# The first layer's two-bank PSUM tile as two one-bank tiles, with every ELU pass done by halves

## The chip, the cores and the metric

One NeuronCore of one Trainium2 chip runs the whole program. A core has five engines with in-order instruction queues of their own: TensorE (PE, matrix multiplication), VectorE (DVE), ScalarE (ACT), GpSimd (POOL) and SyncE (SP, which here only issues DMAs). They meet through semaphores. PE writes its results into PSUM, which has eight banks; a bank holds 512 fp32 values in each of 128 partitions. The metric is the device time of one execution in microseconds (us), the median over repeated runs without a profiler.

## The reference

The input x has 8 batches of 3008 rows and 256 columns. Two parts follow each other.

```
X  = rfft(x, axis=1)                    # along the 3008 rows
Yr = Xr @ w_r - Xi @ w_i + b_r ;  Yi = Xr @ w_i + Xi @ w_r + b_i
Y  = soft threshold of both parts by 0.01
y  = irfft(Y)                           # [8, 3008, 256]

h  = y.reshape(24064, 256) @ w_in       # [24064, 2048], the first layer
g  = where(h > 0, h, exp(min(h, 0)) - 1)  # ELU
out = g @ w_out                         # [24064, 256], the second layer
```

The change lies wholly in the second part: in where h stands in PSUM, and in how the ELU is cut into instructions.

## The kernel before

The Fourier transforms are matrix multiplications in two stages each way, cut into small pieces called units. Unit A is the first stage of the forward transform, X the second, M the complex weights with bias and threshold, B and Y the two stages back. Each unit is a handful of matmuls into PSUM and an evacuation to SBUF by ACT or DVE (line 144 for DVE, line 146 for ACT, in the helper `evac`); M units also use POOL (lines 301 to 303).

The two dense layers are one long loop of 376 steps (line 1207), 47 for each batch. The 24064 rows are taken in blocks of 512 (`TB`), and a block's 2048 hidden columns in eight pairs of 128-column tiles. Step i has these parts:

- `front(i)`: the first layer of one pair. Four bf16 matmuls (line 1006), two for each 128-column tile, write `hps`, a PSUM tile of two banks with one 128-column tile in each. Then ACT computes the exponential of h into `Et` in SBUF.
- `finish_elu()` for the step before: DVE joins `Et` and h to `gT` (line 1048 or 1050). This is the last reader of `hps`, so it frees the banks.
- `elu(i)`: for some steps POOL or DVE limits `Et` (lines 1059 and 1061).
- `back(i - 2)`: the second layer of the pair of two steps earlier, eight fp32 matmuls (line 1080) into `ps_o`. After the eighth pair the block is copied out (line 1092) and stored.

In between, a plan (`plan`, line 1110) places the units of the next batch, one a step, ahead of `front` in the same step (list `f0`) or after `finish_elu` (list `f1`). So the order in every queue is fixed by the program text: PE does unit, first layer, second layer; DVE does the unit's evacuation, then gT of the step before; ACT does the unit's evacuation, then the exponential. Nothing is reordered by a scheduler.

The ELU comes in three ways, chosen by the step's mode:

- "act" steps (130 of them, among them all with M units): ACT computes Relu(-h) into `Et` (line 1024), then Exp(-Et) in place (line 1025), each over both tiles in one instruction of 1024 elements a partition; gT is one DVE instruction of 1024.
- pooled steps (217, among them the first ten, `FILL`, and the calm ones without units): ACT computes Exp by halves of 512 (line 1022), POOL limits each half (line 1059), gT is two DVE instructions of 512.
- plain steps (29): ACT computes Exp over 1024 (line 1027), DVE limits it (line 1061), gT is one DVE instruction of 1024 (line 1050).

PSUM has eight banks: two for `ps_o`, four for `psH` (two tiles of two banks, used in turn), and two that are lent, through `last_banks`, either to the pool `psF` (one two-bank tile for A, X, B and Y units) or to `psM` (two one-bank tiles, for M units). When a calm stretch has no units, every third step's `hps` goes into these last two banks, from `psF` ("third"). The first ten steps are an exception: their h stands in two one-bank tiles `sps`, and each half's Exp is written right behind its own two matmuls (line 1013).

```
hps = psH.tile([P, 2, TB], F32, name="hps", tag="hps")          # line 994
...
nc.scalar.activation(E_, hps[:], AF.Relu, scale=-1.0)           # line 1024
nc.scalar.activation(E_, E_, AF.Exp, scale=-1.0)                # line 1025
...
nc.vector.scalar_tensor_tensor(o, e, -1.0, h, ALU.add, ALU.max) # line 1048
```

Of the kernel before, what the change touches and what calls it, by code (L numbers as in the profile page):

```python
# [8 lines left out]
ALU = mybir.AluOpType  # L9
AF = mybir.ActivationFunctionType  # L10
BF16 = mybir.dt.bfloat16
F32 = mybir.dt.float32
# [17 lines left out]
def kernel(  # L30
# [11 lines left out]
    nc = tc.nc  # L42
    P = nc.NUM_PARTITIONS
# [33 lines left out]
    space = constp.tile([P, 384], BF16, name="space")  # L77
# [13 lines left out]
    TB = 512  # L91
# [4 lines left out]
    n = B * PER  # L96
# [29 lines left out]
    def last_banks(name):  # L126

        if name not in open_pool:
            for _, stack in open_pool.values():
                stack.close()  # L130
            open_pool.clear()
            stack = ctx.enter_context(ExitStack())
            pool = stack.enter_context(
                tc.tile_pool(
                    name=name, bufs=1 if name == "psF" else 2,
                    space=bass.MemoryType.PSUM, reuse_waits="tile",
                )
            )
            open_pool[name] = pool, stack
        return open_pool[name][0]  # L140
# [91 lines left out]
    def three_weights(c, dt):  # L232

        v, r = (w[:, dt, D * c : D * c + D] for w in (wcat_s, wcat_r))
        a, b_ = (r, v) if c else (v, r)
        nc.gpsimd.tensor_tensor(v, a, b_, ALU.subtract)
# [174 lines left out]
    def two_banks(pool, n):  # L411
        return [pool.tile([P, 512], F32, name=n, tag=n) for _ in range(2)]
# [149 lines left out]
    with tc.tile_pool(name="stagep", bufs=1) as stagep:  # L562
# [3 lines left out]
        def col(eng, src, s1, op0, s2=None, op1=None, n=1, dt=F32):  # L566
            t = stagep.tile([P, n], dt, name=f"c{len(cols)}")
            cols.append(t)
            if op1 is None:
                eng.tensor_scalar(t[:], src[:], s1, None, op0)  # L570
            else:
                eng.tensor_scalar(t[:], src[:], s1, s2, op0, op1)
            return t

        def mix(eng, a, sc, b, op0, op1, n=1):
            t = stagep.tile([P, n], F32, name=f"c{len(cols)}")
            cols.append(t)
            eng.scalar_tensor_tensor(t[:], a[:], sc, b[:], op0, op1)
            return t
# [81 lines left out]
        c1 = mix(dve, qcol, -2.0, pcol, ALU.mult, ALU.add)  # L661
        c0 = col(dve, c1, -1.0, ALU.mult, 1.0, ALU.add)
# [307 lines left out]
    FILL = 10  # L970
# [5 lines left out]
    def pieces(t, k):  # L976

        out_, c = [], 0
        while c < k:
            b, r = divmod(t + c, S)  # L980
            e = min(k, c + S - r)
            out_.append((b, r, c, e))
            c = e
        return out_

    def front(i, third, on_act, halves):
        blk, fp = divmod(i, NPAIR)
        early = i < FILL
        if early:
            hps = two_banks((psS0, psS1)[i % 2], "sps")  # L990
        elif third:
            hps = last_banks("psF").tile([P, 2, TB], F32, name="hps", tag="fps")
        else:
            hps = psH.tile([P, 2, TB], F32, name="hps", tag="hps")
        todo = []
        for s in range(2):
            ft = 2 * fp + s
            for piece in sorted(pieces(blk * TB, TB), key=lambda z: z[3] - z[2]):
                todo.append((s, ft, piece))
        if i == PER // NPAIR * NPAIR:  # L1000
            todo.sort(key=lambda z: z[2][0])
        Et = late3.tile([P, 2, TB], F32, name="Et", tag="Et")
        E_ = Et[:]
        for s, ft, (b, t0, c0, c1) in todo:
            for dt in range(2):
                nc.tensor.matmul(  # L1006
                    hps[s][:, c0:c1] if early else hps[:, s, c0:c1],
                    lhsT=w_in_s[:, dt, ft * P : ft * P + P],
                    rhs=yT_of[b][:, dt, t0 : t0 + c1 - c0],
                    start=(dt == 0), stop=(dt == 1),  # L1010
                )
            if early and (dt, c1) == (1, TB):
                nc.scalar.activation(E_[:, s], hps[s][:], AF.Exp)
        if early:
            return hps, Et
        if i == n - 1:
            for h in range(2):
                t = slice(TB // 2 * h, TB // 2 * h + TB // 2)
                nc.scalar.activation(E_[:, :, t], hps[:, :, t], AF.Exp)
        elif halves:  # L1020
            for s in range(2):
                nc.scalar.activation(E_[:, s], hps[:, s], AF.Exp)  # L1022
        elif on_act:
            nc.scalar.activation(E_, hps[:], AF.Relu, scale=-1.0)  # L1024
            nc.scalar.activation(E_, E_, AF.Exp, scale=-1.0)  # L1025
        else:
            nc.scalar.activation(E_, hps[:], AF.Exp)  # L1027
        return hps, Et

    late_elu = []  # L1030
    np_all = (slice(0, P), slice(0, 2), slice(0, TB))

    def parts(i):

        if i == n - 1:
            return [
                (slice(0, P), slice(0, 2), slice(h, h + TB // 2)) for h in (0, TB // 2)
            ]
        return [(slice(0, P), s, slice(0, TB)) for s in range(2)]

    def finish_elu():
        for i, hps, Et, whole, halves in late_elu:
            gT = late3.tile([P, 2, TB], F32R, name="gT", tag="gT")
            for s in parts(i) if halves else (np_all,):
                h = hps[s[1]][:] if i < FILL else hps[s]
                o, e = gT[s], Et[s]
                if whole:
                    nc.vector.scalar_tensor_tensor(o, e, -1.0, h, ALU.add, ALU.max)  # L1048
                else:
                    nc.vector.scalar_tensor_tensor(o, h, 0.0, e, ALU.max, ALU.add)  # L1050
            g_of[i] = gT
        late_elu.clear()

    def elu(i, hps, Et, on_pool, on_act):

        E_ = Et[:]
        if on_pool:
            for s in parts(i):
                nc.gpsimd.tensor_scalar(E_[s], E_[s], 1.0, 0.0, ALU.min, ALU.max)  # L1059
        elif not on_act:  # L1060
            nc.vector.tensor_scalar(E_, E_, 1.0, -1.0, ALU.min, ALU.add)
        late_elu.append((i, hps, Et, on_pool or on_act, on_pool))

    def back(i, split):
        blk, fp = divmod(i, NPAIR)
# [140 lines left out]
    early_h = None  # L1206
    for i in range(n + LAG):
        if i == FILL:
            few.close()
            psH = ctx.enter_context(  # L1210
                tc.tile_pool(
                    name="psH", bufs=2, space=bass.MemoryType.PSUM, reuse_waits="tile"
                )
            )
        if i == LAG:
            back(0, False)
        if early_h:
            h, on_act = early_h, False
        elif i < n:
            r = i % PER  # L1220
            if r == 0:
                f0, f1, mode = plan(i // PER)
                used = [bool(u0 or u1) for u0, u1 in zip(f0, f1)]
            free = not used[r]
            bare = bare + 1 if free else 0
            calm = free and (i >= n - 2 or (r + 2 < PER and not used[r + 1] and not used[r + 2]))
            for f, a in f0[r]:
                f(*a)
            if mode[r]:
                on_act = mode[r] == "act"  # L1230
                pooled = not on_act
            else:
                on_act = any(f is unit_M for f, a in f0[r])
                pooled = free or i < FILL
            third = calm and bare % 3 == (2 if i // PER == B - 1 else 1)
            h = front(i, third, on_act, pooled)
        finish_elu()
        if i < n:
            for f, a in f1[r]:
                f(*a)  # L1240
            split = i > LAG and (i - LAG) % NPAIR == NPAIR - 1
            if split:
                back(i - LAG, True)
            elu(i, *h, pooled, on_act)
            if PER <= i < PER + 4:
                three_weights(*divmod(i - PER, 2))
            if 1 <= i < 5:
                if i < 3:
                    scale_w_in(2, True, i - 1)
                scale_w_in(3, False, (i - 1) // 2, (i - 1) % 2)  # L1250
            if i == n - 2:
                early_h = front(n - 1, True, False, True)
            elif early_h:
                early_h = None
        else:
            split = False
        if i > LAG and not split:
            back(i - LAG, False)
# [30 lines left out]
```

## Time and profile before

| what | value |
|---|---|
| median of 3 runs without a profile | 894.95 us (894.54 to 895.38) |
| span of the profiled execution, first to last instruction | 903.9 us |
| PE matmul busy | 891.3 us (99%), 6917 matmuls |
| PE weight loads busy | 675.2 us (75%) |
| DVE busy | 679.6 us (75%), 969 instructions |
| ACT busy | 722.4 us (80%), 1001 instructions |
| POOL busy | 596.7 us (66%), 806 instructions |
| mean granted PE clock | 0.948 |

The profile is of one execution; its only time on record is the span, which is longer than the runs without a profile. Busy time of PE is the union of its matmuls' modelled durations, which overlap: a matmul of 512 columns is listed with 390 ns, though the next one may start earlier. In the rows of the timeline the columns are the start and the duration in us, the engine, the source line, the operation, what it writes and reads, how many equal instructions in a row are merged, and in brackets the idle time of the engine before it with what ended it. In the rows of the groups, the number behind "x" is the count, then come busy time in us, mean ns of one instruction, and idle time ahead of them with its causes.

### The profile page before, as it was taken

How to read it: one execution, taken by the hardware profiler on the slowest of the kernel's cores; microseconds unless marked ns; L12 is line 12 of the kernel's file. 1: busy time of each engine (PE TensorE's matmuls, PEld its weight loads, DVE VectorE, ACT ScalarE, POOL GpSimd, SP SyncE). 2: the span in 40 equal slices, each digit the busy share in tenths (PEclk: the TensorE clock that was granted, in tenths of full speed). 3: DMA queues.
4: the chain of work that ended last, by engine and by line, in shares of the span. 5: the costliest groups of instructions: out<-in, count | busy, mean ns of one | idle time of the engine just before them, and what ended most of it. 6: DMA issues, size and time to landing. Idle time of an engine off the chain costs nothing.

```text
span 903.9 us, 18292 instructions
## 1 busy us (share of the span) xinstructions
PE 891.3 (99%) x6917; PEld 675.2 (75%) x6917; DVE 679.6 (75%) x969; ACT 722.4 (80%) x1001; POOL 596.7 (66%) x806
## 2 busy tenths in 40 slices
PE   9999999999999999999999999999999999999997
PEld 3467667877788777877778777787777877777776
DVE  7788778688866887668866788677876678778776
ACT  6778778888978889798887988878887798776654
POOL 7562550788657886588756877559875697753664
PEclk9999999999999999999999999999999999999998
DMA  8996226631474115632265231643218201241111
GB/s 262 310 258 188 70 71 181 169 119 47 118 209 124 65 50 152 173 117 88 72 181 136 86 116 48 189 140 101 87 53 229 70 24 48 69 108 36 28 44 47
DMA packets 90718, 105.85 MB, mean 117 GB/s; under 512 B 5395, under 2 KB 81174, under 8 KB 87302
## 3 DMA queue, kind: packets, MB, share of 16 engines
q1 hardware_dynamic: 84278, 76.64, 30.0%
q0 software_dynamic: 5968, 27.26, 9.4%
q8 instruction: 54, 0.88, 0.4%
q10 hardware_dynamic: 384, 0.79, 0.3%
q14 instruction: 34, 0.28, 0.1%
HBM read 54.86 MB, written 49.81 MB: 116 GB/s over the span
## 4 chain that ended last, share of the span: by engine, by line
PE 90%; DVE 3%; DMA 3%; ACT 2%; POOL 1%; issue 1%; SPq 0%; DVEq 0%; ACTq 0%; POOLq 0%
PE ps_o L1080 37%; PE hps L1006 36%; PE mps L289 5%; PE bps L375 2%; PE xps L207 2%; PE yps L538 2%; PE aps L170 2%; DVE gT L1048 2%; PE mps L247 1%; DVE Bz L144 1%; DMA xt<-in_x_dram 1%; DMA Z<-DA 1%; DMA DB<-Bz 1%; PE sps L1006 1%; DMA DA<-A 0%
## 5 line engine op out<-in xcount | busy, mean ns | idle before, releaser
L1048 DVE SCALAR_TENSOR_TENSOR gT<-Et,hps 128x512 fp32r<-128x512 f32 (+1 forms) x544 | 423.7, 811 | 158.5 <-POOL Et L1059 115.4
L1080 PE MATMUL ps_o<-w_out_r,gT 128*128 128x256 f32 x3008 | 481.4, 303 | 0.0
L1080 PEld LDWEIGHTS ps_o<-w_out_r,gT 128*128 128x128 f32 x3008 | 407.7, 190 | 52.4 <-ACT osb L1092 0.5
L1059 POOL TENSOR_SCALAR Et<-Et 128x512 f32<-128x512 f32 x434 | 258.3, 614 | 223.6 <-ACT Et L1022 213.2
L1006 PE MATMUL hps<-yT,w_in_s 128*128 128x512 bf16 (+7 forms) x1688 | 388.9, 360 | 2.0 <-DVE gT L1048 1.3
L1022 ACT ACTIVATE Et<-hps 128x512 f32<-128x512 f32 x412 | 224.2, 598 | 67.8 <-PE hps L1006 63.3
L1006 PEld LDWEIGHTS <-w_in_s 128*128 128x128 bf16 x1728 | 144.7, 99 | 119.7 <-issue 21.7
L1024 ACT ACTIVATE Et<-hps 128x1024 f32<-128x1024 f32 x130 | 133.6, 1027 | 57.3 <-PE hps L1006 49.0
L1025 ACT ACTIVATE Et<-Et 128x1024 f32<-128x1024 f32 x130 | 137.4, 1057 | 4.1
L301 POOL TENSOR_TENSOR yb<-yb,bias_bc 128x512 f32<-128x512 f32 x72 | 92.3, 1282 | 9.5 <-DVE yb L296 9.4
L303 POOL TENSOR_TENSOR Y<-yb,clip 128x512 bf16<-128x512 f32 x72 | 92.6, 1286 | 6.0
L296 DVE TENSOR_TENSOR yb<-mps,yb 128x512 f32<-128x512 f32 x72 | 49.8, 692 | 7.6 <-PE hps L1006 0.5
L146 ACT CAST XT<-xps 128x768 bf16<-128x768 f32 x57 | 45.5, 799 | 9.8 <-PE xps L207 9.7
L146 ACT CAST A<-aps 128x1024 bf16<-128x1024 f32 x40 | 40.5, 1014 | 11.4 <-PE aps L170 9.9
L302 POOL TENSOR_SCALAR clip<-yb 128x512 f32<-128x512 f32 x72 | 44.2, 614 | 6.3
L289 PE MATMUL mps<-wcat_s,XT 128*128 128x256 bf16 x288 | 44.1, 277 | 0.0
L144 DVE COPY yb<-mps 128x256 f32<-128x256 f32 x72 | 30.3, 421 | 11.1 <-PE mps L289 9.7
L1050 DVE SCALAR_TENSOR_TENSOR gT<-hps,Et 128x1024 fp32r<-128x1024 f32 x29 | 35.5, 1223 | 2.4
L224 POOL TENSOR_TENSOR XS<-XT 128x512 bf16<-128x512 bf16 x30 | 34.1, 1159 | 2.1 <-ACT XT L146 1.2
L1092 DVE COPY osb<-ps_o 128x512 f32<-128x512 f32 x46 | 31.6, 686 | 1.2 <-PE ps_o L1080 0.5
L146 ACT CAST Bz<-bps 128x1024 bf16<-128x1024 f32 x32 | 31.9, 998 | 0.5 <-PE bps L375 0.4
L1027 ACT ACTIVATE Et<-hps 128x1024 f32<-128x1024 f32 x29 | 29.8, 1029 | 2.6 <-PE hps L1006 1.2
(184 smaller groups left out, 678.8 us busy)
## 6 DMA issues: line engine op xcount, KB each, us to landing
xt<-in_x_dram POOLq DMA_DIRECT2D x21, 1024.0 KB, 5.4
out_dram<-osb SPq DMA_DIRECT2D x158, 128.0 KB
Bs<-DB SPq DMA_DIRECT2D x30, 384.0 KB
DB<-Bz SPq DMA_DIRECT2D x20, 512.0 KB
DA<-A SPq DMA_DIRECT2D x19, 512.0 KB
Z<-DA SPq DMA_DIRECT2D x5, 1152.0 KB
Z<-DA SPq DMA_DIRECT2D x11, 384.0 KB
xt<-in_x_dram POOLq DMA_DIRECT2D x6, 512.0 KB, 6.0
```

Source lines behind the costliest of these rows:

```text
L146: nc.scalar.copy(dst, src)
L289: nc.tensor.matmul(out_, lhsT=lhs[:, dt] if lhs is not None else sum_of(dt, ch)[:, oc : oc + P], rhs=w[:, dt, :], start=(dt == 0), stop=(d ...
L296: nc.vector.tensor_tensor(yb[:].rearrange("p (c d) -> p c d", c=2), ps[:].rearrange("p (c d) -> p c d", c=2), yb[:, D : 2 * D].unsqueeze(1 ...
L301: nc.gpsimd.tensor_tensor(yb[:], yb[:], bias_bc[:], ALU.add)
L303: nc.gpsimd.tensor_tensor(Y_of[b, q][:, i, :], yb[:], clip[:], ALU.subtract)
L1006: nc.tensor.matmul(hps[s][:, c0:c1] if early else hps[:, s, c0:c1], lhsT=w_in_s[:, dt, ft * P : ft * P + P], rhs=yT_of[b][:, dt, t0 : t0 + ...
L1022: nc.scalar.activation(E_[:, s], hps[:, s], AF.Exp)
L1024: nc.scalar.activation(E_, hps[:], AF.Relu, scale=-1.0)
L1025: nc.scalar.activation(E_, E_, AF.Exp, scale=-1.0)
L1048: nc.vector.scalar_tensor_tensor(o, e, -1.0, h, ALU.add, ALU.max)
L1059: nc.gpsimd.tensor_scalar(E_[s], E_[s], 1.0, 0.0, ALU.min, ALU.max)
L1080: nc.tensor.matmul(po[q][:, i_ % 2, :], lhsT=gT[:, s, i_ * P : i_ * P + P], rhs=w_out_r[:, ft, :], start=(ft == 0 and i_ % 2 == 0), stop=( ...
```

## The change

Every step's h now stands in two one-bank tiles, except the very last step's, which keeps its two-bank tile: `psH` has four one-bank buffers in place of two of two banks, and "third" steps take two tiles of `psM` in place of one of `psF`. In act and plain steps each pass of ACT over 1024 elements is two of 512, and gT is two DVE instructions of 512. The first pass of each half (Relu in act steps, Exp in the others) is written directly behind that half's own matmuls; in act steps the two Exp follow both Relu. DVE's limiting pass of the plain steps stays one instruction of 1024. The first ten steps and the last stay as they were. The order of the instructions in each queue is otherwise the same, and the numbers of matmuls, of POOL's instructions and of DMAs don't change.

```diff
-    def front(i, third, on_act, halves):
+    def front(i, third, on_act):
         blk, fp = divmod(i, NPAIR)
-        early = i < FILL
-        if early:
+        last = i == n - 1
+        if i < FILL:
             hps = two_banks((psS0, psS1)[i % 2], "sps")
+        elif last:
+            pair = last_banks("psF").tile([P, 2, TB], F32, name="hps", tag="fps")
+            hps = [pair[:, s, :] for s in range(2)]
         elif third:
-            hps = last_banks("psF").tile([P, 2, TB], F32, name="hps", tag="fps")
-        else:
-            hps = psH.tile([P, 2, TB], F32, name="hps", tag="hps")
+            hps = two_banks(last_banks("psM"), "mps")
+        else:
+            hps = two_banks(psH, "hps")
+        hps = [h if last else h[:] for h in hps]
...
+        left = [len(todo) // 2] * 2
         Et = late3.tile([P, 2, TB], F32, name="Et", tag="Et")
-        E_ = Et[:]
         for s, ft, (b, t0, c0, c1) in todo:
             for dt in range(2):
                 nc.tensor.matmul(
-                    hps[s][:, c0:c1] if early else hps[:, s, c0:c1],
+                    hps[s][:, c0:c1],
...
-            if early and (dt, c1) == (1, TB):
-                nc.scalar.activation(E_[:, s], hps[s][:], AF.Exp)
-        if early:
-            return hps, Et
-        if i == n - 1:
+            left[s] -= 1
+            if left[s] or last:
+                continue
+            if on_act:
+                nc.scalar.activation(Et[:, s], hps[s], AF.Relu, scale=-1.0)
+            else:
+                nc.scalar.activation(Et[:, s], hps[s], AF.Exp)
+        if on_act:
+            for s in range(2):
+                nc.scalar.activation(Et[:, s], Et[:, s], AF.Exp, scale=-1.0)
...
-        elif halves:
-            for s in range(2):
-                nc.scalar.activation(E_[:, s], hps[:, s], AF.Exp)
-        elif on_act:
-            nc.scalar.activation(E_, hps[:], AF.Relu, scale=-1.0)
-            nc.scalar.activation(E_, E_, AF.Exp, scale=-1.0)
-        else:
-            nc.scalar.activation(E_, hps[:], AF.Exp)
-        return hps, Et
...
     def finish_elu():
-        for i, hps, Et, whole, halves in late_elu:
+        for i, hps, Et, whole in late_elu:
             gT = late3.tile([P, 2, TB], F32R, name="gT", tag="gT")
-            for s in parts(i) if halves else (np_all,):
-                h = hps[s[1]][:] if i < FILL else hps[s]
-                o, e = gT[s], Et[s]
+            for t, s, h, e in parts(i, hps, Et):
+                o = gT[:, s, t]
...
-                    name="psH", bufs=2, space=bass.MemoryType.PSUM, reuse_waits="tile"
+                    name="psH", bufs=4, space=bass.MemoryType.PSUM, reuse_waits="tile"
```

`two_banks(pool, n)`, which was there before (line 411), takes two tiles of one bank each from a pool.

More of the change, by code (lines that the diff above doesn't have):

```diff
@@ L1011, in front, with parts @@
                 )
-            if early and (dt, c1) == (1, TB):
-                nc.scalar.activation(E_[:, s], hps[s][:], AF.Exp)
-        if early:
-            return hps, Et
-        if i == n - 1:
+            left[s] -= 1
[8 more added lines that the diff above has]
+                nc.scalar.activation(Et[:, s], Et[:, s], AF.Exp, scale=-1.0)
+        if last:
             for h in range(2):
                 t = slice(TB // 2 * h, TB // 2 * h + TB // 2)
-                nc.scalar.activation(E_[:, :, t], hps[:, :, t], AF.Exp)
-        elif halves:
-            for s in range(2):
-                nc.scalar.activation(E_[:, s], hps[:, s], AF.Exp)
-        elif on_act:
-            nc.scalar.activation(E_, hps[:], AF.Relu, scale=-1.0)
-            nc.scalar.activation(E_, E_, AF.Exp, scale=-1.0)
-        else:
-            nc.scalar.activation(E_, hps[:], AF.Exp)
+                nc.scalar.activation(Et[:, :, t], pair[:, :, t], AF.Exp)
+            hps = pair
         return hps, Et
     late_elu = []
-    np_all = (slice(0, P), slice(0, 2), slice(0, TB))
-    def parts(i):
+    def parts(i, hps, Et):
         if i == n - 1:
[L1036 to L1039, printed above, removed]
+            for h in (0, TB // 2):
+                t = slice(h, h + TB // 2)
+                yield t, slice(0, 2), hps[:, :, t], Et[:, :, t]
+        else:
+            for s in range(2):
+                yield slice(0, TB), s, hps[s], Et[:, s]
     def finish_elu():
-        for i, hps, Et, whole, halves in late_elu:
+        for i, hps, Et, whole in late_elu:
             gT = late3.tile([P, 2, TB], F32R, name="gT", tag="gT")
-            for s in parts(i) if halves else (np_all,):
-                h = hps[s[1]][:] if i < FILL else hps[s]
-                o, e = gT[s], Et[s]
+            for t, s, h, e in parts(i, hps, Et):
+                o = gT[:, s, t]
                 if whole:
@@ L1054, in elu @@
     def elu(i, hps, Et, on_pool, on_act):
-        E_ = Et[:]
         if on_pool:
-            for s in parts(i):
-                nc.gpsimd.tensor_scalar(E_[s], E_[s], 1.0, 0.0, ALU.min, ALU.max)
+            for t, s, h, e in parts(i, hps, Et):
+                nc.gpsimd.tensor_scalar(e, e, 1.0, 0.0, ALU.min, ALU.max)
         elif not on_act:
-            nc.vector.tensor_scalar(E_, E_, 1.0, -1.0, ALU.min, ALU.add)
-        late_elu.append((i, hps, Et, on_pool or on_act, on_pool))
+            nc.vector.tensor_scalar(Et[:], Et[:], 1.0, -1.0, ALU.min, ALU.add)
+        late_elu.append((i, hps, Et, on_pool or on_act))
     def back(i, split):
@@ L1235 @@
             third = calm and bare % 3 == (2 if i // PER == B - 1 else 1)
-            h = front(i, third, on_act, pooled)
+            h = front(i, third, on_act)
         finish_elu()
@@ L1251 @@
             if i == n - 2:
-                early_h = front(n - 1, True, False, True)
+                early_h = front(n - 1, True, False)
             elif early_h:
```

## The prediction

> **What bounds the kernel now.** I read the page's shares and clock first, then the groups by shape, the waits, and last the timeline of single steps ("step" is one turn of the main loop: one pair of first-layer tiles, 376 in all).
>
> ```profile
> span 903.9 us, 18292 instructions
> PE   9999999999999999999999999999999999999997
> PEclk9999999999999999999999999999999999999998
> PE 90%; DVE 3%; DMA 3%; ACT 2%; POOL 1%; issue 1%; SPq 0%; DVEq 0%; ACTq 0%; POOLq 0%
> ```
>
> TensorE (PE) is busy in every slice and carries 90% of the chain that ended last. The profiled span is 903.9 us, 8.95 us over the median 894.95 of the runs without a profile; nothing shown divides those 8.95 us, so I work out a difference in the profile and take it off the median unscaled.
>
> Busy PE can still hide short waits, because a matmul's modelled end lies past the start of the next. Start to start tells more. A calm step, with no Fourier unit in it:
>
> ```profile
> 846.04 1.28 PE L1080 MATMUL ps_o<-w_out_r,gT 128*128 128x256 f32 x8
> 847.16 1.06 PE L1006 MATMUL hps<-yT,w_in_s 128*128 128x512 bf16 x4
> 847.76 1.29 DVE L1048 SCALAR_TENSOR_TENSOR gT<-Et,hps 128x512 fp32r<-128x512 f32 x2 [0.55 <-POOL Et L1059]
> 847.86 1.29 PE L1080 MATMUL ps_o<-w_out_r,gT 128*128 128x256 f32 x8
> 848.99 1.06 PE L1006 MATMUL hps<-yT,w_in_s 128*128 128x512 bf16 x4
> ```
>
> From one first-layer group to the next are 1.83 us, and from eight second-layer matmuls to the next first layer 1.12. Four first-layer matmuls last 1.06 with the last one's 0.39 (the mean in the next fence), so they start (1.06 - 0.39)/3 = 0.22 apart: the second half tile's first matmul comes 0.45 after the first half's. These are PE's own rates; the change removes no matmul. All that it can win is PE's waits.
>
> ```profile
> L1006 PE MATMUL hps<-yT,w_in_s 128*128 128x512 bf16 x1240 | 329.1, 390 | 1.9 <-DVE gT L1048 1.3
> L1048 DVE SCALAR_TENSOR_TENSOR gT<-Et,hps 128x512 fp32r<-128x512 f32 x414 | 265.7, 683 | 115.6 <-POOL Et L1059 115.4
> L1022 ACT ACTIVATE Et<-hps 128x512 f32<-128x512 f32 x412 | 224.2, 598 | 67.8 <-PE hps L1006 63.3
> L1048 DVE SCALAR_TENSOR_TENSOR gT<-Et,hps 128x1024 fp32r<-128x1024 f32 x130 | 158.0, 1215 | 43.0 <-ACT Et L1025 43.0
> L1025 ACT ACTIVATE Et<-Et 128x1024 f32<-128x1024 f32 x130 | 137.4, 1057 | 4.1
> L1024 ACT ACTIVATE Et<-hps 128x1024 f32<-128x1024 f32 x130 | 133.6, 1027 | 57.3 <-PE hps L1006 49.0 <-DVE yb L296 5.5 <-DVE yT L144 0.2
> L1050 DVE SCALAR_TENSOR_TENSOR gT<-hps,Et 128x1024 fp32r<-128x1024 f32 x29 | 35.5, 1223 | 2.4
> ```
>
> The groups name one releaser of the first layer: gT on VectorE (DVE), the instruction that frees the PSUM pair. The group view counts 1.9 us of such idle time; starts show more. Here are the first and the last of the waits that I counted, and the largest two kinds:
>
> ```profile
> 139.05 0.63 PE L170 MATMUL aps<-xt,M 128*128 128x512 f32 x2
> 139.64 1.06 PE L1006 MATMUL hps<-yT,w_in_s 128*128 128x512 bf16 x4
> 141.46 0.62 PE L170 MATMUL aps<-xt,M 128*128 128x512 f32 x2
> 141.93 0.39 PE L1006 MATMUL hps<-yT,w_in_s 128*128 128x512 bf16 x1
> ...
> 519.76 1.21 DVE L1048 SCALAR_TENSOR_TENSOR gT<-Et,hps 128x1024 fp32r<-128x1024 f32 x1
> 520.16 0.61 PE L289 MATMUL mps<-wcat_s,XT 128*128 128x256 bf16 x4
> 521.02 1.05 PE L1006 MATMUL hps<-yT,w_in_s 128*128 128x512 bf16 x4 [0.25 <-DVE gT L1048]
> ...
> 782.20 1.23 DVE L144 CAST Bz<-bps 128x1024 bf16<-128x1024 f32 x1 [0.50 <-PE bps L375]
> 782.79 1.29 PE L1080 MATMUL ps_o<-w_out_r,gT 128*128 128x256 f32 x8
> 783.34 1.21 DVE L1048 SCALAR_TENSOR_TENSOR gT<-Et,hps 128x1024 fp32r<-128x1024 f32 x1
> 784.61 1.07 PE L1006 MATMUL hps<-yT,w_in_s 128*128 128x512 bf16 x4 [0.53 <-DVE gT L1048]
> ...
> 820.11 1.28 PE L1080 MATMUL ps_o<-w_out_r,gT 128*128 128x256 f32 x8
> 821.44 1.06 PE L1006 MATMUL hps<-yT,w_in_s 128*128 128x64 bf16 x8
> ```
>
> The first: 0.59 from the unit's matmuls to the first layer where the next step has 0.47, so 0.12 lost. The last: 1.33 where a calm step has 1.12, so 0.21. At 784.61 it is 1.82 against 1.12, 0.69 lost, and the start follows the end of gT (784.55). At 521.02 it is 0.86 against the 0.45 of other such steps (302.31 to 302.76 below): 0.42 lost. Counted so over all steps after the tenth, 43 first-layer groups start over 0.04 us late, by 7.05 us in sum; 0.68, 0.69 and 0.42 are the largest, the rest lie under 0.23. One of 0.23 waits for ACT, not for gT.
>
> **The change part by part.**
>
> *Release by halves.* Each half tile is a bank of its own and is free when its own half of gT is done. In "act" steps (130 Relu-Exp pairs) and the 29 plain ones, gT was one instruction of 1.215 us; as two, a pair lasts 265.7/207 = 1.283 and its second costs 1.283 - 0.683 = 0.60 at the margin. So the first half comes free 1.215 - 0.683 = 0.53 earlier (0.6 by the margin), the second 0.07 later, but the second is needed 0.45 later too. A wait of x becomes max(0, x - 0.38). In steps whose gT was already in halves, the pair waited for the second; there it becomes x - 0.45. Of the 43 waits, three keep something: 0.04 + 0.30 + 0.31 = 0.65.
>
> *Earlier exponentials.* Before, even a half's Exp began only after all four matmuls. An act step with an M unit:
>
> ```profile
> 302.31 0.61 PE L289 MATMUL mps<-wcat_s,XT 128*128 128x256 bf16 x4
> 302.51 0.42 DVE L144 COPY yb<-mps 128x256 f32<-128x256 f32 x1
> 302.76 1.06 PE L1006 MATMUL hps<-yT,w_in_s 128*128 128x512 bf16 x4
> 303.04 0.69 DVE L296 TENSOR_TENSOR yb<-mps,yb 128x512 f32<-128x512 f32 x1
> 303.65 1.21 DVE L1048 SCALAR_TENSOR_TENSOR gT<-Et,hps 128x1024 fp32r<-128x1024 f32 x1
> 303.86 1.03 ACT L1024 ACTIVATE Et<-hps 128x1024 f32<-128x1024 f32 x1 [0.41 <-PE hps L1006]
> 304.92 1.06 ACT L1025 ACTIVATE Et<-Et 128x1024 f32<-128x1024 f32 x1
> 305.28 1.06 PE L1006 MATMUL hps<-yT,w_in_s 128*128 128x512 bf16 x4
> ```
>
> The Relu begins 1.10 after the group; the first half's would begin 0.45 sooner. I count nothing for it here: gT stands behind the M unit's two DVE instructions and begins when they end (303.65), not when Exp does (302.39 + 1.06 = 303.45).
>
> *ACT's added instructions.* 2 x 130 + 29 = 289 more. From PSUM a pair of halves lasts 224.2/206 = 1.09 against 1.027: +0.06. The pass Et to Et is nowhere split before; nearest rows bound it by +0.06 (the pair just named) and 2 x 0.598 - 1.057 = +0.14; less than zero is excluded, since the elements stay the same. I take +0.06, a back-to-back pair being what it will be. An act step then costs ACT 1.09 + 1.12 = 2.21 (at most 2.39), and PE needs 2.52 (302.76 to 305.28). In all about 130 x 0.12 + 29 x 0.06 = 17 us of ACT, at cost nothing: the cover is the 0.41 of idle time before each Relu. Without the cover, each 0.1 us over 2.52 costs up to 13 us in 130 steps.
>
> [...]
>
> *DVE's added instructions.* 159 more, +0.07 each (1.283 against 1.215), bounded above by 2 x 0.683 - 1.215 = +0.15. An M step then holds 0.42 + 0.69 + 1.28 = 2.39 (at most 2.48) of 2.52: hidden, but near. Behind gT on DVE stand the next M unit's copy and the output copy. Where waits follow each other closely (steps around 521 us: 0.08, 0.42, 0.08) DVE sets the pace, and half a tile's head start pays once, not for each; I take off 0.2.
>
> *More waits on PE.* By the instruction lists of both programs 526 full-width first-layer matmuls wait for DVE instead of 255. The first ten steps already have the new layout:
>
> ```profile
> 58.64 1.21 PE L1006 MATMUL sps<-yT,w_in_s 128*128 128x512 bf16 x4 [0.57 <-DVE gT L1048]
> 61.11 1.07 PE L1006 MATMUL sps<-yT,w_in_s 128*128 128x512 bf16 x4
> ```
>
> Where the second half's wait has to last, the group shows it (1.21); where it is met, the group takes 1.07, as the undivided ones do (1.05 to 1.07). I take nothing; the rounding allows 271 x 0.01 = 2.7 us either way.
>
> *Third pair from the M pool.* It takes the same two banks. In the calm step above gT ends at 849.05 and the pair comes up again three steps on (847.16 - 1.83 + 5.5 = 850.8): 1.8 us to spare, and no queue is passed. No DMA, no POOL instruction and no matmul moves; the last step keeps its two-bank tile. These cost nothing.
>
> Sum: 7.05 - 0.23 (for ACT) - 0.65 - 0.2 = 6.0 us. In the profile 903.9 becomes 897.9; the runs go from 894.95 to 889.0.
>
> **The rivals.**
>
> *DVE becomes the pace (slower).* If two halves of gT don't overlap as the mean says and cost 1.37, an M step holds 2.48, and the output copy of 0.69 once in eight steps makes it 2.56, over PE's 2.52. The point is a pair of 1.32. Each of 130 act steps then loses 0.04 and nothing is won: 894.95 + 5.2 = 900.2. For it: DVE is the releaser of every wait above, and its act steps get longer. Against it: the pair's 1.283 is a mean over 207.
>
> *The waits come back (no change).* PE reaches the next wait sooner and stays there, because DVE's lateness is that of its own queue, or because the second half's extra 0.07 always ends last: 893.2 to 896.7. For it: the waits near 521 us come in threes. Against it: most are single, 5 to 30 us apart, and both follow a gT that DVE began late for one reason only.
>
> [...]
>
> **How the numbers follow.** The forecast (886.5 to 891.5) has 0.58; ACT full 0.05, no change 0.17, DVE's pace 0.20. A run of this kernel tells 0.2% (1.8 us) from no change. So faster 0.63, same 0.17, slower 0.20. The floor is all 7.05 won, 887.9, less rounding: low 887.4. The range reaches through the no-change case into the slower one, to 897.5, which leaves about 0.12 above and 0.06 below.
>
> **What would show it.** In the changed profile: first-layer starts follow the group before at 0.45, 0.47 and 1.12 nearly everywhere, the 0.69 waits shrink to 0.3; Relu or Exp halves begin about 0.65 after their group's start instead of 1.10; ACT is near 740 us busy, DVE near 690, PE's chain share up. I am wrong if gT's pairs in act steps take over 1.32, if the four ACT passes take over 2.5, if the first layer's groups get longer than 1.07 (the second half waiting inside the group), or if the PE clock falls.

## The result, and the profile after

The changed kernel takes 885.12 us (median of 4, 884.78 to 886.39) where the kernel before takes 895.15 (median of 4): a ratio of 0.9894, 95% interval 0.9880 to 0.9908. That is 10.0 us less by the medians and 9.5 by the ratio, where 6.0 were forecast (889.0, range 887.4 to 897.5): the direction was right, and the time lies 2.3 us below the range. On two other occasions, each with both kernels on one chip, the change won 8.95 and 9.10 us by the medians (last row of the table below), also more than was forecast.

The first lines of the page, for the changed kernel:

```profile
span 884.6 us, 18406 instructions
PE 866.4 (98%) x6813; PEld 666.4 (75%) x6917; DVE 690.1 (78%) x1128; ACT 723.1 (82%) x1290; POOL 597.1 (68%) x806
PEclk9999999999999999999999999999999999999999
PE 92%; DVE 2%; DMA 2%; ACT 1%; issue 1%; POOL 1%; SPq 0%; DVEq 0%; POOLq 0%
```

PE still carries nearly all of the chain. The granted clock is 0.999 here and was 0.948 in the profile that the prediction read; that profile is of an execution at a lower clock than the runs that were timed, so the spans 903.9 and 884.6 can't be subtracted from each other. A second profile of the kernel before (first experiment) has a clock of 0.998 and a span of 893.9, and the comparison below goes by that one. DVE's share of the chain is 4% there and 2% here.

The groups that the change made or split, by shape; the first line is gT's in the act steps of the kernel before (second profile), the others are of the changed kernel:

```profile
L1048 DVE SCALAR_TENSOR_TENSOR gT<-Et,hps 128x1024 fp32r<-128x1024 f32 x130 | 158.0, 1215 | 42.2 <-ACT Et L1025 42.2
...
L1051 DVE SCALAR_TENSOR_TENSOR gT<-Et,hps 128x512 fp32r<-128x512 f32 x626 | 398.4, 682 | 110.4 <-POOL Et L1061 103.5 <-ACT Et L1025 6.3
L1010 PE MATMUL hps<-yT,w_in_s 128*128 128x512 bf16 x1070 | 293.8, 380 | 5.6 <-DVE gT L1051 0.8
L1025 ACT ACTIVATE Et<-Et 128x512 f32<-128x512 f32 x260 | 149.8, 633 | 0.0
L1020 ACT ACTIVATE Et<-hps 128x512 f32<-128x512 f32 x260 | 141.6, 598 | 43.6 <-PE hps L1010 33.2 <-PE mps L289 7.9 <-PE bps L375 1.3
```

gT's idle time behind ACT fell from 42.2 us (the row of the 130 undivided gT) to 6.3: the halves of Exp are mostly there when DVE comes to them. 104 of the 6917 matmul records are missing from this trace (rows with x3 where x4 is meant); where a count of waits needs them, their place is read from the neighbours.

The place of the longest waits, an act step with a B unit. The timeline of PE and DVE, kernel before (second profile), then the kernel after:

```profile
774.28 1.22 DVE L144 CAST Bz<-bps 128x1024 bf16<-128x1024 f32 x1 [0.41 <-PE bps L375]
774.85 1.28 PE L1080 MATMUL ps_o<-w_out_r,gT 128*128 128x256 f32 x8
775.42 1.21 DVE L1048 SCALAR_TENSOR_TENSOR gT<-Et,hps 128x1024 fp32r<-128x1024 f32 x1
776.69 1.04 PE L1006 MATMUL hps<-yT,w_in_s 128*128 128x512 bf16 x4 [0.55 <-DVE gT L1048]
```

```profile
765.15 1.23 DVE L144 CAST Bz<-bps 128x1024 bf16<-128x1024 f32 x1 [0.38 <-PE bps L375]
765.73 1.28 PE L1082 MATMUL ps_o<-w_out_r,gT 128*128 128x256 f32 x8
766.30 2.47 DVE L1051 SCALAR_TENSOR_TENSOR gT<-Et,hps 128x512 fp32r<-128x512 f32 x4
767.03 1.19 PE L1010 MATMUL hps<-yT,w_in_s 128*128 128x512 bf16 x4
```

Before, the first layer starts 1.84 us after the second layer's group; at this clock the same two stand 1.11 apart in calm steps (835.32 and 836.43 in that trace), so 0.73 is lost, and the start comes 0.06 behind the end of gT. After, it is 1.30, and the start comes 0.73 behind the begin of gT, when one half is done; the other wait shows as a group of 1.19 where 1.02 to 1.04 are usual, its second half held up by about 0.17.

### The profile page after: what moved, and what is told of

Its sections match the earlier page's. It is cut to its first block, busy times and chain, and to the rows that moved or that the text cites. A ratio compares the mean times of both kernels' runs of the same rounds, so it can differ in the third digit from the quotient of the medians.

```text
span 884.6 us, 18406 instructions
## 1 busy us (share of the span) xinstructions
PE 866.4 (98%) x6813; PEld 666.4 (75%) x6917; DVE 690.1 (78%) x1128; ACT 723.1 (82%) x1290; POOL 597.1 (68%) x806
## 4 chain that ended last, share of the span: by engine, by line
PE 92%; DVE 2%; DMA 2%; ACT 1%; issue 1%; POOL 1%; SPq 0%; DVEq 0%; POOLq 0%
PE ps_o L1082 39%; PE hps L1010 33%; PE mps L289 5%; PE bps L375 3%; PE mps L1010 2%; PE xps L207 2%; PE yps L538 2%; PE aps L170 2%; PE mps L247 1%; PE sps L1010 1%; DVE gT L1051 1%; DMA Z<-DA 1%; DMA xt<-in_x_dram 1%; ACT A L146 0%; DMA DA<-A 0%
## 5 line engine op out<-in xcount | busy, mean ns | idle before, releaser
L1051 DVE SCALAR_TENSOR_TENSOR gT<-Et,hps 128x512 fp32r<-128x512 f32 x626 | 398.4, 682 | 110.4 <-POOL Et L1061 103.5
L1082 PE MATMUL ps_o<-w_out_r,gT 128*128 128x256 f32 x3008 | 476.3, 301 | 0.0
L1082 PEld LDWEIGHTS ps_o<-w_out_r,gT 128*128 128x128 f32 x3008 | 403.6, 189 | 48.6 <-ACT osb L1094 1.1
L1010 PE MATMUL hps<-yT,w_in_s 128*128 128x512 bf16 (+6 forms) x1486 | 348.2, 350 | 5.7 <-DVE gT L1051 0.8
L1022 ACT ACTIVATE Et<-hps 128x512 f32<-128x512 f32 x422 | 232.1, 609 | 40.1 <-PE hps L1010 37.2
L1020 ACT ACTIVATE Et<-hps 128x512 f32<-128x512 f32 x260 | 141.6, 598 | 43.6 <-PE hps L1010 33.2
L1025 ACT ACTIVATE Et<-Et 128x512 f32<-128x512 f32 x260 | 149.8, 633 | 0.0
L1053 DVE SCALAR_TENSOR_TENSOR gT<-hps,Et 128x512 fp32r<-128x512 f32 x58 | 37.3, 685 | 2.4
L1051 DVE SCALAR_TENSOR_TENSOR gT<-Et,mps 128x512 fp32r<-128x512 f32 x48 | 30.8, 684 | 8.6 <-POOL Et L1061 8.6
L146 ACT CAST yT<-yps 128x752 bf16<-128x752 f32 x34 | 26.7, 787 | 12.7 <-PE yps L538 12.3
L1022 ACT ACTIVATE Et<-mps 128x512 f32<-128x512 f32 x48 | 26.1, 599 | 12.2 <-PE mps L1010 11.1
```

Source lines behind the costliest of these rows:

```text
L146: nc.scalar.copy(dst, src)
L1010: nc.tensor.matmul(hps[s][:, c0:c1], lhsT=w_in_s[:, dt, ft * P : ft * P + P], rhs=yT_of[b][:, dt, t0 : t0 + c1 - c0], start=(dt == 0), sto ...
L1020: nc.scalar.activation(Et[:, s], hps[s], AF.Relu, scale=-1.0)
L1022: nc.scalar.activation(Et[:, s], hps[s], AF.Exp)
L1025: nc.scalar.activation(Et[:, s], Et[:, s], AF.Exp, scale=-1.0)
L1082: nc.tensor.matmul(po[q][:, i_ % 2, :], lhsT=gT[:, s, i_ * P : i_ * P + P], rhs=w_out_r[:, ft, :], start=(ft == 0 and i_ % 2 == 0), stop=( ...
```

## The experiments

Waits ahead of the first layer are counted as in the prediction, from start to start, in the steps after the first 80 us whose four matmuls have full width (about 305; steps that cross a batch border are left out), over 0.04 us each. A wait of the second half, which shows inside the group, counts as one too. Where records are missing, a group that starts late by just one missing matmul ahead of it isn't counted. "Ratio" is to the kernel before on the same chip; 894.35 is the median of 19 runs of it beside the second profile, whose own execution took 895.95.

| kernel | waits | sum, us | time, us | ratio, 95% interval |
|---|---|---|---|---|
| before, profile of the prediction (clock 0.948) | 37 | 6.35 | | |
| before, second profile (clock 0.998) | 53 | 9.57 | 894.35 | 1 |
| passes split, two-bank tiles kept | 54 | 11.41 | 896.35 | 1.0022 (1.0013 to 1.0031) |
| release as a whole | 54 | 10.96 | 895.21 | 1.0014 (1.0005 to 1.0024) |
| release by halves behind pooled steps alone | 45 | 8.95 | 893.38 | 0.9991 (0.9981 to 1.0000) |
| second half first, banks pinned | 46 | 8.85 | 891.57 | 0.9978 (0.9968 to 0.9988) |
| release by halves behind act and plain steps alone | 16 | 3.13 | 887.46 | 0.9928 (0.9912 to 0.9943) |
| late first passes | 8 | 1.00 | 886.35, 886.04 | 0.9918 (0.9901 to 0.9934), 0.9908 (0.9894 to 0.9922) |
| second half first | 7 | 1.02 | 885.80 | 0.9904 (0.9888 to 0.9921) |
| one Exp of 1024 | 4 | 0.67 | 884.91 | 0.9893 (0.9879 to 0.9906) |
| changed kernel | 8 | 0.91 | 884.91, 885.26 | 0.9899 (0.9884 to 0.9914), 0.9897 (0.9883 to 0.9911) |

**The kernel before, profiled again.** No edit.

> The unchanged kernel before, for a second profile: is the granted clock of 0.948 its own, or that of one execution? Theory A (the profile that the prediction read was of an execution at a lower clock than the runs; at the full clock PE asks for its banks sooner, so the same DVE instructions make it wait longer): clock near 1.00, span 893 to 894 us, the waits ahead of the first layer near 10 us instead of 7.05. Theory B (the clock of 0.948 belongs to the kernel before, and its denser or looser PE stream is what the change altered): clock 0.948 again, span near 904 us, waits near 7 us.

Theory A holds: the clock is 0.998. The timed runs of the kernel before beside these experiments list 0.997 to 1.000 as well. The page and the waits:

```profile
span 893.9 us, 18292 instructions
PE 879.8 (98%) x6917; PEld 670.3 (75%) x6917; DVE 679.8 (76%) x969; ACT 722.2 (81%) x1001; POOL 596.0 (67%) x806
PE 91%; DVE 4%; ACT 2%; DMA 2%; issue 1%; POOL 0%; DVEq 0%; SPq 0%; ACTq 0%; POOLq 0%
PE hps L1006 <- DVE gT L1048: 2.0, 6, 0.6
```

The same program with the same instructions on DVE, ACT and POOL (busy times within 0.7 us) has DVE at 4% of the chain instead of 3%, and in the prediction's count, over all steps, 59 waits of 10.55 us instead of 43 of 7.05. At the higher clock PE comes to its banks sooner (a calm step takes 1.80 us, 834.63 to 836.43 in that trace, where it took 1.83), DVE frees them no sooner (gT takes 683 and 1215 ns in both), and the waits grow; 16 more come above 0.04 us. So the profile that the prediction read showed PE more nearly the bound than it is in the runs that are timed.

**Release by halves alone.** Every first pass after the tenth step waits for the step's last matmul:

```diff
-            if on_act:
-                nc.scalar.activation(Et[:, s], hps[s], AF.Relu, scale=-1.0)
-            else:
-                nc.scalar.activation(Et[:, s], hps[s], AF.Exp)
+        if not last and i >= FILL:
+            for s in range(2):
+                if on_act:
+                    p = nc.scalar.activation(Et[:, s], hps[s], AF.Relu, scale=-1.0)
+                else:
+                    p = nc.scalar.activation(Et[:, s], hps[s], AF.Exp)
+                if s == 0:
+                    dep(mm, p)
```

`dep(mm, p)` makes `p` wait for the step's last matmul.

> The changed kernel, but the first pass of each step (after the tenth) waits for all four matmuls of the step: release by halves alone, no earlier exponential. If release by halves carries the gain: 885 to 887 us. If the earlier exponentials carry it: 892 to 895 us.

> Release by halves alone (the first passes wait for all four matmuls), again, beside the changed kernel on one chip. If the earlier exponentials are worth nothing, as the sum had it: equal to the changed kernel within 0.5 us. If they carry what the two earlier runs on different chips differ by (0.9918 against 0.9894 and 0.9899 of before): 1.5 to 2 us slower than it.

Nearly all of the gain is still there: 886.35, and 886.04 beside 885.26 of the changed kernel on one chip, which is between the two expectations of the second run. The 0.8 us between them lie inside the intervals, so that the early exponentials win anything beside release by halves isn't shown.

**Early exponentials alone.** A step's first matmul waits for the second half of gT of the step that held the pair:

```diff
+                if i >= FILL and not last and (s, ft, dt) == (*todo[0][:2], 0):
+                    if len(users) >= (1 if third else 2) and c0 == todo[0][2][2]:
+                        behind(mm, second_half[users[-1 if third else -2]])
```

> The changed kernel, but a step's first matmul waits until both halves of the pair before it are free: earlier exponentials alone, no release by halves. If release by halves carries the gain: 891 to 895 us. If the earlier exponentials carry it: 885 to 887 us.

Against the kernel before nothing of the gain is left, 1.0014. The waits of that kernel:

```profile
PEld L1010 <- DVE gT L1066: 19.3, 65, 0.8
PE hps L1010 <- DVE gT L1066: 3.2, 10, 0.8
```

Here the wait stands ahead of the first weight load. Neither row is the loss itself: from start to start 10.96 us are lost. PE's own row shows less than that (at 776.69 above 0.55 where 0.73 were lost), and a weight load's idle time in that trace holds more than the wait (0.21 at 775.07, put down to gT, where the same 0.21 at 780.11 is put down to no other engine). In the changed kernel no weight load waits for gT, and one row is left in this view, which leaves out the shortest waits:

```profile
PE hps L1010 <- DVE gT L1051: 0.8, 1, 0.8
```

It is new and stands at the first step after the first ten, where the pools change from `sps` to `psH`: the second half tile there waits 0.9 us, once (it starts at 74.73, 1.14 behind the matmul before it where 0.22 is usual; the table's count begins later, at 80 us). Why it does was not followed up.

**The added instructions alone.** The kernel before with its tiles, and ACT's and DVE's passes of act and plain steps by halves:

```diff
-            nc.scalar.activation(E_, hps[:], AF.Relu, scale=-1.0)
-            nc.scalar.activation(E_, E_, AF.Exp, scale=-1.0)
+            for s in range(2):
+                nc.scalar.activation(E_[:, s], hps[:, s], AF.Relu, scale=-1.0)
+            for s in range(2):
+                nc.scalar.activation(E_[:, s], E_[:, s], AF.Exp, scale=-1.0)
...
-            for s in parts(i) if halves else (np_all,):
+            for s in parts(i):
```

> The kernel before with its two-bank tiles, but with ACT's and DVE's passes of act and plain steps by halves: the added 289 and 159 instructions alone, without either benefit. If they are hidden, as the sum had it: 895 to 896 us. If DVE or ACT becomes the pace (the slower rival): 898 to 901 us, first-layer waits longer by 0.07 to 0.15 each.

They cost 2.0 us (1.2 to 2.8), more than "hidden" and less than the rival. The waits grow from 9.57 to 11.41 in about as many places: the tail of each pair of gT is what the next first layer waits for, and it ends later (a pair takes 1.28, the undivided gT took 1.215). This kernel is the base of the two before it, and all three ran on one chip: release by halves alone takes it from 896.35 to 886.35, 10.0 us, and the early exponentials alone take it to 895.21, 1.1 us less, which lies inside the intervals. So release by halves wins 10 us, and 2 of them pay for the added instructions.

**Which waits count.** Release by halves behind one kind of step alone; behind the other kind the pair is released as a whole, as in the third experiment:

```diff
+                        prev = users[-1 if third else -2]
+                        if pooled_of[prev]:
+                            behind(mm, second_half[prev])
```

The other run has `if not pooled_of[prev]:`.

> The changed kernel again, beside the next two on one chip. Of the waits of the second profile of before (59, 10.55 us) those left should be few: the earlier run with late first passes kept 10, of 2.2 us. Expected 0.989 to 0.990 of before, and 1 to 2 us of waits ahead of the first layer.

> The changed kernel, but a pair whose last user was a pooled step (gT was in two instructions already) is released as a whole: release by halves only behind act and plain steps. In the second profile of before 43 waits of 7.7 us followed a gT of 1024 and 15 of 2.6 us one of 512. If each wait counts by itself: about 2.6 us over the changed kernel, 887 to 888.5. If the waits behind pooled steps are only the tail of lateness from act steps: within 1 us of the changed kernel.

> The changed kernel, but a pair whose last user was an act or plain step is released as a whole: release by halves only behind pooled steps. If each wait counts by itself, 7.7 us over the changed kernel and up to 2 more for the longer pairs of gT: 892 to 895. If the longer lateness only moves on to pooled steps and is met there by their halves: 887 to 890.

887.46 and 893.38 beside 884.91: +2.6 and +8.5, where the waits counted singly gave 2.6 and 7.7 to 9.7. Each wait counts by itself; those behind pooled steps aren't a tail of the others.

**The second Exp pass in one instruction.**

```diff
-            for s in range(2):
-                nc.scalar.activation(Et[:, s], Et[:, s], AF.Exp, scale=-1.0)
+            nc.scalar.activation(Et[:], Et[:], AF.Exp, scale=-1.0)
```

> The changed kernel with the second pass of act steps (Exp, Et to Et) in one instruction of 1024 again: 130 ACT instructions fewer, but the first half of gT now waits for the whole Exp. If DVE's own queue sets when gT begins: within 0.5 us of the changed kernel. If ACT is the near limit (the ACT rival): up to 1 us faster for its 0.09 us a step; if gT's begin hangs on the first Exp half: 1 to 3 us slower.

> The changed kernel beside these two on the same chip: 0.989 to 0.990 of before.

884.91 beside 885.26: no difference clear of the noise, and 0.67 us of waits beside 0.91. ACT isn't near a limit, and the first half of Exp isn't what gT waits for, though gT's row in that kernel shows the wait that it gives up:

```profile
L1050 DVE SCALAR_TENSOR_TENSOR gT<-Et,hps 128x512 fp32r<-128x512 f32 x626 | 400.5, 682 | 123.9 <-POOL Et L1060 97.9 <-ACT Et L1024 25.8
```

25.8 us behind ACT instead of 6.3, and the time is no longer for it.

**The order of release, without an added wait.** Release as a whole had been made with waits that stood ahead of the weight loads: 297 first-layer weight loads carried one, and 6 in the changed kernel. To tell the order of release from that, gT takes the second half first:

```diff
-            for s in range(2):
+            for s in (1, 0):
                 nc.scalar.activation(Et[:, s], Et[:, s], AF.Exp, scale=-1.0)
...
-            for t, s, h, e in parts(i, hps, Et):
+            order = list(parts(i, hps, Et))
+            for t, s, h, e in order if pooled_of[i] else order[::-1]:
```

> The changed kernel, but in act and plain steps the second half goes first through gT (and through the second Exp pass), so that the bank needed first comes free last, with no wait added anywhere. If the order of release is the whole of it: like release as a whole behind those steps, 892 to 895 us. If the earlier run of that kind lost its time because its added waits stood ahead of the weight loads: 885 to 887 us.

885.80, as fast as the changed kernel, against my theory as it stood. The reason is in the banks: the pool gives the bank that comes free first to the first tile that asks, so the halves had changed places (159 of 339 pairs in the allocation). With banks of their own for each half:

```diff
-            hps = two_banks(psH, "hps")
+            hps = [psH.tile([P, 512], F32, name="hps", tag=f"hps{s}") for s in range(2)]
...
-                    name="psH", bufs=4, space=bass.MemoryType.PSUM, reuse_waits="tile"
+                    name="psH", bufs=2, space=bass.MemoryType.PSUM, reuse_waits="tile"
```

> As the run before (second half first through gT in act and plain steps), but each half keeps banks of its own, so that the first half of a step can only take a bank that a first half held. In the run before, the pool's allocation gave the bank that came free first to the first half: by the allocation lists 159 of 339 pairs were exchanged, and the order of release was not changed at all. Now the bank needed first comes free last behind act and plain steps, and no wait is added anywhere; 7 first-layer weight loads carry a wait, as in the changed kernel. If the order of release is the whole of it: 892 to 895 us. If release as a whole was slow only for its waits ahead of the weight loads: 885 to 887 us.

891.57, 46 waits of 8.85 us. The place shown above, in this kernel:

```profile
771.05 2.47 DVE L1052 SCALAR_TENSOR_TENSOR gT<-Et,hps 128x512 fp32r<-128x512 f32 x4
772.38 1.02 PE L1010 MATMUL hps<-yT,w_in_s 128*128 128x512 bf16 x4 [0.61 <-DVE gT L1052]
```

PE starts 1.33 behind the begin of gT, after both halves, where the changed kernel starts 0.73 behind it. So the order of release alone makes 6.3 to 6.7 us (by the ratios about 7) of the 8.5 that release as a whole behind act and plain steps cost; it came out 0.4 below what was expected. The waits of the two kernels are alike (8.85 and 8.95). Their times, taken on different chips, differ by 1.8 us and by the ratios by 1.2, with intervals that overlap; whether the added waits cost anything of their own isn't shown.

## Why the prediction was right or wrong

*What bounds the kernel* was right in kind: PE's waits for gT's release are what the change won. After it 0.91 us of them are left of 9.57.

*The size failed at one step*: "I work out a difference in the profile and take it off the median unscaled". The profiled span lay 8.95 us over the median, and the page gave the clock as 0.948; the prediction left that open and took the waits from that execution. At the clock of the timed runs the term "7.05" is 10.55, and the floor of the range, "all 7.05 won", was no floor. Put into the prediction's own sum: 10.55 less 0.25 for ACT, less what stays. By x - 0.38, the waits of 0.72, 0.71 and 0.48 keep 0.34, 0.33 and 0.10; with the 0.2 for pace 0.97 stays (0.91 was counted). That gives 9.3 us won and, from 895.15, 885.8 us, 0.7 above what was measured. The wait of 0.9 us at the change of pools, which the prediction didn't have, goes the other way: with it the sum is 8.4 us, and the measured gains are 10.0, 8.95 and 9.10. Where the other 0.5 to 1.6 us come from isn't shown.

*The law of a wait*, max(0, x - 0.38): the 0.73 above left 0.17 at the first half and 0.17 at the second, 0.34 in sum where the law gives 0.35. At the step of the 0.48 nothing over 0.04 is left, where the law gives 0.10.

*The 0.2 for pace* came out. Apart from the two places of 0.34, four waits are left, each 0.06 at a second half (groups of 1.08 and 1.09 at 405.67, 512.57, 619.54 and 726.52), 0.24 in sum. The waits that stood there before were under 0.38, but each followed another closely; the one at 512.57 stands in the step behind that of the 0.48.

*Earlier exponentials at nothing*: right to within about 1 us, by the medians. Release by halves alone is 0.8 us behind the changed kernel, and on top of the split passes they won 1.1 us; neither is clear of the noise. The first layer's waits are 1.00 us without them and 0.91 with them, which fits the reason given, that gT stands behind other work of DVE.

*ACT's added instructions at nothing*: right, and dearer in the sum than on the chip. An act step of the changed kernel:

```profile
295.11 1.03 PE L1010 MATMUL hps<-yT,w_in_s 128*128 128x512 bf16 x4
295.40 0.69 DVE L296 TENSOR_TENSOR yb<-mps,yb 128x512 f32<-128x512 f32 x1
295.74 1.09 ACT L1020 ACTIVATE Et<-hps 128x512 f32<-128x512 f32 x2 [0.33 <-PE hps L1010]
296.01 1.28 DVE L1051 SCALAR_TENSOR_TENSOR gT<-Et,hps 128x512 fp32r<-128x512 f32 x2
296.71 1.15 ACT L1025 ACTIVATE Et<-Et 128x512 f32<-128x512 f32 x2
```

The first Relu begins 0.63 behind its group's start, as was forecast. The four passes take 2.12 us from first start to last end (295.74 to 297.86); the two before took 2.12 as well (303.86 to 305.98 in the prediction's rows). There the second began 0.03 behind the end of the first; here the pairs, 1.09 and 1.15, overlap by 0.12. 2.21 was forecast; ACT's busy time is 723.1, not 740. That the cover was ample also shows in the run with one Exp, where 130 instructions fewer changed nothing. The pairs last 0.15 more than the single passes (1.09 and 1.15 against 1.03 and 1.06); the overlap of 0.12, and 0.03 that stood between the single ones, take that up.

*DVE's added instructions at nothing*: the price was right (a pair 1.28, 690.1 us busy against "near 690"), but "hidden" was not. In the old layout they cost 2.0 us together with ACT's (the two weren't tested apart), as longer waits for gT. With release by halves these waits are gone, as the prediction's 0.45 of head start for the second half has it.

*More waits on PE at nothing*: right. A first-layer group with all its waits met lasts 1.02 to 1.04 in both kernels at this clock.

*The rivals*: DVE as the pace fell (a pair costs 1.28, under the point of 1.32, and the time went down). That the waits come back fell: the two kinds of wait add up singly. ACT full (0.05), by which the added instructions would have cost ACT more than PE leaves it in a step, fell: with one instruction less in each act step the time was 884.91 beside 885.26.

## What to carry to other kernels

Before a duration or a wait is taken from a profile, compare its span and its granted clock with the timed runs. Here the waits of the engine that the clock slowed, for one that it didn't slow, were too short in the profile (7.05 against 10.55; first-layer matmuls 0.224 us apart against 0.216, gT 683 ns at either clock), and the gain from removing them was underestimated. Where the refill of a two-bank buffer that is filled and drained by halves waits for the drain, release by halves is worth a try: here half a refill of head start took the waits from 53 to 8 (9.57 to 0.91 us) and paid for the longer passes. To test an order of release, pin the buffers: here the allocation by first release undid the edit (159 of 339 pairs exchanged, 885.80 us; pinned, 891.57).

## What the runs showed of the hardware

The granted clock of a kernel that runs on one core was 0.948 on average in one execution (0.95 in each of five stretches between 22.6 and 860 us) and 0.997 to 1.000 on average in all later profiles of this study. With the clock 5% higher the span of the same kernel was only 1.1% shorter (903.9 to 893.9), with waits that were 3.5 us longer. First-layer matmuls of 512 columns start a median of 0.224 us apart at 0.948 and 0.216 at 0.999 (the changed kernel's profile), 3.6% less; the second layer's fp32 ones of 256 columns start a median of 0.118 apart in both. DVE, ACT and POOL kept their durations in the two profiles of the kernel before: 683 and 1215 ns for gT, 1027 for Relu and 1057 for Exp of 1024, 614 for POOL's limit. What set the clock of 0.948 is open.
